# One attention and MLP kernel: the halves of the first MLP tiles placed block by block, and all order tables remade

## The chip, the cores and the metric

The kernel runs on one core of one Trainium2 chip. The metric is the time of one execution on the device, in microseconds. Each core has TensorE (PE, matmuls and transposes; PEld is its weight load), VectorE (DVE), ScalarE (ACT), GpSimd (POOL) and SyncE (SP, which here only issues DMAs). Each engine works through its own instructions strictly in order, and waits for others by semaphores.

## What is computed

```python
# attention: q, k, v (2, 8, 768, 64), centroids (8, 16, 64)
q_assign = argmax(q_n . c_n); k_assign = argmax(k_n . c_n)      # nearest of 16 centroids, by cosine
scores = where(q_assign == k_assign, q . k / 8, -1e9)
x = softmax(scores) @ v                                         # heads side by side: (1536, 512)
# first MLP, weights (512, 2048) and (2048, 512)
h = x @ w_in;  x = (h * cos(h)) @ w_out
# second MLP, weights of the same shapes
h = x @ w_in;  out = where(h > 0, h, exp(min(h, 0)) - 1) @ w_out
```

The MLP weights arrive as 64-bit floats.

## The kernel before, in words

Products of 32-bit precision are made of rounded parts: a value is split into a high half (a copy rounded to the type fp32r that TensorE takes) and a low half (the value less the high half), and a product is the sum of three matmuls, high by high, high by low and low by high.

Attention goes by pairs of heads (8 pairs), each of 12 steps, a step being 128 query rows of one head: 96 steps in all (`NS`). A step n has score matmuls (`qk`, lines 746 and 749, tile s), the row maximum on VectorE (`rowmax`, L754), the exponent on ScalarE (`expo`, L760), six transposes on TensorE (`turn`, L769), the high halves of these on ScalarE (`p_hi`, L783) and the low halves on VectorE (`p_lo`, L789). After three steps twelve value matmuls follow (`av`, L800), which two ScalarE copies (`x_low`, `x_main`, L842 and L853), two GpSimd passes (`x_add`, `x_mul`) and the reciprocal of the row sums (`den_eps`, `recip`, then by way of DRAM `recip_rows` and `recip_out` on SP) turn into x. Beside it the next pair is made ready: transposes of raw q and k (`raw_pe`, L445) and their halves, similarities with the centroids (`sims_pe`, L586, one matmul per 128 rows), sums, a maximum and a first-of-equals (`sims_*`, `best`, `assign` which writes M), and a mask (`mask_pe`, `mask_out`). For the first pair this stands ahead of everything, head by head (`first_*`, L499 to L519; `square` and `sum_sq` for the norms).

An MLP goes by three tiles of 512 tokens (t) and in each by 16 blocks of 128 hidden columns (f). `g1` makes h of a block with 12 matmuls (L203), `act` makes the activation and its halves GH and GL, `g2` adds the block's part to four accumulators with 12 matmuls (L262). In the first tile of each MLP the weights are made too, as `w_part(m, f, i)`: i = 0 a ScalarE pass over the raw words into u (L145), i = 1 a shift and i = 2 a merge on VectorE (L147, L149), i = 4 the high half (`whi`, L82 where ScalarE has it), i = 5 the low half (`wlo`, L157 where GpSimd has it), each of 128x1024. The raw words of a block's weights, 1 MB, come by two DMAs (L130, L132) into the slot that the halves fill later; the first MLP's slots 0 to 4 are loaded in `open_mlp`, 5 to 15 in `close_attention`, which stands behind all of attention in SP's queue. There are two buffers for u, so block f waits for the low half of the block two before it. `act` of the first MLP is: i = 0 h plus a constant on ScalarE (A), i = 2 the remainder on VectorE (R), i = 3 its absolute value on VectorE (`ABS_ON`), i = 4 Sin on ScalarE, i = 5 the product with h on VectorE, i = 6 the high half GH (`GHI_ON`) and i = 7 the low half GL (`GLO_ON`). `finish` takes an accumulator out, and in the second MLP sends it to DRAM.

The order on each engine is that of a list of parts with a time each: the tables `FIRST` (first pair), `PAIR`, `STEP`, `HALF`, `UNIT` (the steady part of attention), `LAST` (the handover from attention to the MLP) and `MLP` give every part a time in steps, the list is sorted by it, and the parts issue their instructions in that order. The times decide nothing but this order. Which engine does a part is read from the tables that end in `_ON`; `OWN` can overrule them for one block:

```python
def place(what, *key):
    return OWN.get((what, *key))
...
copy_on(place("whi", m, f) or WHI_ON[m], slots[m, f][:, 0:WCOLS], f32(w_u[m, f]))
...
if (place("abs", t, f) or ABS_ON[min(t, 1)]) == "act":
    nc.scalar.activation(out=R, in_=R, func=AF.Abs)
```

Before, `OWN` is empty: in the first tile of the first MLP ScalarE makes all weight high halves and GH, GpSimd all weight low halves and GL, VectorE all absolute values; in that of the second MLP GpSimd makes GH as well.

Of the kernel before, what the change touches and what calls it, by code (L numbers as in the profile page):

```python
# [27 lines left out]
UNIT = {'den_eps': 3.395449, 'recip': 4.382076, 'recip_rows': 7.427179, 'recip_out': 8.211055, 'x_add': 9.795484, 'x_mul': 13.848315}  # L30
LAST = {'open_mlp': (-10.431815,), 'x_hi': (-9.514192, -7.034133, -2.555486, -10.023157), 'x_lo': (-8.047097, -4.932345, -0.617305, -2.950232), 'w_part:0': (-9.420448, -8.609347, -8.290691, -5.915885, -5.184987, -2.504884), 'w_part:1': (-8.653788, -6.829189, -4.664081, -3.78072, -2.797147, -1.733981), 'w_part:2': (-2.317206, -1.232418, -0.87148, -0.600955, 0.212419, 3.118759), 'w_part:3': (-0.448697, 0.124409, 0.564191, 2.438164, 2.488768, 4.597908), 'g1': (-0.307886, 1.731051, 4.372541, 5.094428), 'close_attention': (5.33528,), 'act:0': (0.747785, 0.837811, 1.046582, 2.277094, 3.196946, 3.362042, 3.445046, 4.730737), 'act:1': (2.594399, 2.876142, 3.118762, 3.599105, 4.068132, 4.163887, 5.689334, 7.654582), 'act:2': (4.468217, 4.516452, 5.198942, 5.360867, 5.778692, 5.82839, 5.899724, 7.733904), 'act:3': (6.073842, 6.854719, 7.291519, 7.399848, 7.722534, 7.931365, 8.663391, 8.863032), 'g2': (6.668914, 8.520482, 9.303291, 9.815031), 'w_part:4': (2.42712, 2.960527, 3.091453, 3.209423, 3.851579, 6.448056), 'w_part:5': (5.381259, 5.610103, 6.550675, 6.924254, 7.503784, 8.022706), 'w_part:6': (6.555402, 7.031497, 8.030499, 8.308408, 8.684242, 8.926541), 'w_part:7': (9.14231, 9.347017, 9.526266, 9.904052, 10.071843, 10.148753), 'w_part:8': (9.531231, 9.594698, 10.007708, 10.329222, 10.764157, 11.321912), 'w_part:9': (10.67596, 11.080638, 11.588344, 12.058398, 12.098845, 12.307885)}
BASE = 2.147
MLP = ({'w_part:0': -0.40466, 'w_part:1': -0.292589, 'w_part:2': 0.151477, 'w_part:3': 0.670537, 'w_part:4': 0.692693, 'w_part:5': 1.293487, 'g1': 1.795143, 'g2': 5.151129, 'load_w': 11.132613, 'x_hi:0': 1.217665, 'x_lo:0': 1.636338, 'x_hi:1': 0.983316, 'x_lo:1': 1.380274, 'x_hi:2': 0.937158, 'x_lo:2': 1.409528, 'x_hi:3': 0.999253, 'x_lo:3': 1.237302, 'finish:0': 4.421941, 'finish:1': 5.153119, 'finish:2': 4.32082, 'finish:3': 5.26658, 'act:0': 2.239128, 'act:1': 2.366001, 'act:2': 2.377866, 'act:3': 2.492051, 'act:4': 3.000199, 'act:5': 3.084461, 'act:6': 3.139014, 'act:7': 3.424962, 'late_g2:10': 0.47351, 'late_g2:11': 0.529335, 'late_g2:12': 0.229903, 'late_g2:13': -0.690981, 'late_g2:14': -1.391747, 'late_g2:15': -0.882423, 'late_g1:0': 0.043116, 'late_g1:1': -0.794958, 'late_g1:2': -0.713539, 'late_g1:3': 0.294451}, {'w_part:0': -1.966086, 'w_part:1': -1.781932, 'w_part:2': -0.788006, 'w_part:3': -0.687154, 'w_part:4': -0.611143, 'w_part:5': -0.155152, 'g1': 0.285498, 'g2': 4.282268, 'x_hi:0': 1.691513, 'x_lo:0': 1.848892, 'x_hi:1': 0.938852, 'x_lo:1': 1.85853, 'x_hi:2': 1.333847, 'x_lo:2': 2.040859, 'x_hi:3': 0.942491, 'x_lo:3': 1.7925, 'finish:0': 4.212529, 'finish:1': 4.739817, 'finish:2': 5.863002, 'finish:3': 5.213858, 'act:0': 2.365997, 'act:1': 2.670811, 'act:2': 2.797702, 'act:3': 2.855854, 'act:4': 2.922669, 'act:5': 3.098445, 'act:6': 3.341422, 'act:7': 3.474716, 'late_g2:10': -0.3881, 'late_g2:11': -0.322637, 'late_g2:12': 0.583968, 'late_g2:13': -0.381267, 'late_g2:14': -0.649267, 'late_g2:15': -0.687804, 'late_g1:0': 1.985026, 'late_g1:1': 1.123216, 'late_g1:2': 1.16334, 'late_g1:3': 0.760294})
OWN = {}
XLO_ON = {(0, 0): 'pool', (0, 1): 'dve', (0, 2): 'dve', (1, 0): 'dve', (1, 1): 'dve', (1, 2): 'dve'}
GHI_ON = {(0, 0): 'act', (0, 1): 'act', (1, 0): 'pool', (1, 1): 'act'}
GLO_ON = {(0, 0): 'pool', (0, 1): 'pool', (1, 0): 'pool', (1, 1): 'pool'}
RAW_ON = {('k', 0): 'act', ('k', 1): 'dve', ('q', 0): 'act', ('q', 1): 'act'}
HI2_ON = {('k', 0): 'act', ('k', 1): 'act', ('q', 0): 'act', ('q', 1): 'dve'}
ZON = {'z': 'act', 'k': 'act', 'q': 'act'}  # L40
VHI_ON = {0: 'pool', 1: 'pool'}
SS_ON = {'k': 'pool', 'q': 'pool'}
# [13 lines left out]
def kernel(ctx: ExitStack, tc: tile.TileContext, q, k, v, centroids,  # L56
# [229 lines left out]
    with ExitStack() as actx:  # L286
# [724 lines left out]
```

## Time and profile before

| | us |
|---|---|
| median of 3 runs | 809.8 (808.7 to 810.39) |
| the profiled execution | 809.21 |
| its span, first to last instruction | 807.4 |
| busy: PE, PEld | 782.2, 669.3 |
| busy: DVE, ACT, POOL | 465.2, 490.2, 411.3 |

Busy times are of one profiled execution. Matmuls overlap one another and their ends are modelled, so a busy TensorE can still have waited; how much it had to do is seen from the distance of instructions that follow each other without a wait. The stages by time: the first pair's preparation to about 22 us, attention to 277, the first MLP from there (its first matmuls begin at 266.83, between the last steps of attention) and the second to 802.4. The clock of TensorE is given as a share of full speed, 2.4 GHz.

### The profile page before, as it was taken

The page shows a single profiled execution, that of the slowest core. Times are in us where ns is not written, and L with a number is a line of the kernel's source. Part 1 is how long each engine was busy: PE and PEld are TensorE (multiplying, and loading weights), DVE is VectorE, ACT ScalarE, POOL GpSimd, SP SyncE. Part 2 cuts the span into 40 slices and gives each one's busy share as a digit, 9 for nine tenths or more (in the row PEclk, how much of TensorE's full clock was granted, in tenths as well). Part 3 has the DMA queues.
Part 4 walks back from the last instruction along what each step waited for, and adds up shares of the span by engine and source line. Part 5 has one row for each costly group of instructions (what it writes and reads, how often), then busy time and mean ns, then how long its engine had stood idle before and what let it go on. Part 6 is the DMA issues. An engine that isn't in the chain of part 4 may idle for free.

```text
span 807.4 us, 11261 instructions
## 1 busy us (share of the span) xinstructions
PE 782.2 (97%) x4003; PEld 669.3 (83%) x4003; DVE 465.2 (58%) x751; ACT 490.2 (61%) x894; POOL 411.3 (51%) x427
## 2 busy tenths in 40 slices
PE   5999999999998988999999999999999999999997
PEld 4898999999997876888888888888888888888886
DVE  7898899899898767953332443577874111121110
ACT  4798998998999966744433453556563533343332
POOL 3657667667655767942221132379997222123221
PEclk9999999999999998999999999999999999999999
DMA  3645746746736294000000046571000100010001
GB/s 99 148 103 115 182 101 130 176 96 141 173 76 229 64 377 153 1 0 1 1 1 0 1 157 202 178 246 53 1 1 1 52 1 1 0 43 10 0 1 52
DMA packets 62920, 67.99 MB, mean 84 GB/s; under 512 B 30416, under 2 KB 51408, under 8 KB 62864
## 3 DMA queue, kind: packets, MB, share of 16 engines
q1 hardware_dynamic: 62864, 67.28, 29.8%
q8 instruction: 31, 0.51, 0.3%
q14 instruction: 25, 0.20, 0.1%
HBM read 46.17 MB, written 3.19 MB: 61 GB/s over the span
## 4 chain that ended last, share of the span: by engine, by line
PE 81%; DVE 7%; DMA 5%; ACT 3%; POOL 1%; issue 1%; SPq 1%; ACTq 0%; DVEq 0%; POOLq 0%
PE a L262 31%; PE h L203 30%; PE pt L769 6%; PE px L800 5%; PE s L746 3%; PE s L749 3%; DVE m L754 2%; PE pt_sim L586 2%; PE pt_raw L445 1%; DMA raw<-in_moe_w_in_dram 1%; DVE PL L789 1%; DMA R<-row 1%; ACT u L145 1%; POOL slot L157 1%; DMA raw<-in_moe_w_out_dram 1%
## 5 line engine op out<-in xcount | busy, mean ns | idle before, releaser
L245 POOL TENSOR_TENSOR GL<-A,GH 128x512 fp32r<-128x512 f32 x96 | 134.5, 1402 | 271.1 <-ACT GH L82 268.9
L203 PE MATMUL h<-XH,slot 128*128 128x512 f32 x768 | 252.5, 392 | 4.6 <-POOL slot L157 4.4
L203 PEld LDWEIGHTS h<-XH,slot 128*128 128x128 f32 x768 | 145.0, 189 | 36.0 <-POOL slot L157 5.3
L203 PE MATMUL h<-XL,slot 128*128 128x512 f32 x384 | 150.4, 392 | 0.0
L240 DVE SCALAR_TENSOR_TENSOR A<-R,h 128x512 f32<-128x512 f32 x48 | 33.0, 687 | 161.3 <-ACT R L238 151.1
L262 PE MATMUL a<-GH,slot 128*128 128x512 f32 x384 | 125.6, 391 | 0.0
L262 PE MATMUL a<-slot,GH 128*128 128x512 f32 x384 | 118.3, 389 | 0.0
L789 DVE TENSOR_TENSOR PL<-pt,PH 128x384 fp32r<-128x384 f32 x192 | 98.4, 545 | 20.3 <-ACT PH L783 18.7
L82 ACT ACTIVATE GH<-A 128x512 fp32r<-128x512 f32 x80 | 50.5, 631 | 70.4 <-DVE A L234 37.0
L754 DVE TENSOR_REDUCE m<-s 128x1 f32<-128x768 f32 x96 | 91.1, 949 | 3.7 <-PE s L749 2.1
L783 ACT ACTIVATE PH<-pt 128x384 fp32r<-128x384 f32 x192 | 85.8, 494 | 12.1 <-PE pt L769 10.8
L769 PE MATMUL pt<-ident,P 128*128 128x128 f32 x576 | 89.0, 279 | 1.0 <-DVE PL L789 0.7
L760 ACT ACTIVATE P<-s,m 128x768 f32<-128x768 f32 x96 | 87.1, 907 | 3.5 <-DVE m L754 3.1
L157 POOL TENSOR_TENSOR slot<-u,slot 128x1024 fp32r<-128x1024 f32 x32 | 81.0, 2532 | 12.7 <-ACT slot L82 12.5
L262 PEld LDWEIGHTS a<-GH,slot 128*128 128x128 f32 x384 | 72.6, 189 | 15.1
L203 PEld LDWEIGHTS h<-XL,slot 128*128 128x128 f32 x384 | 72.6, 189 | 14.9
L262 PEld LDWEIGHTS a<-slot,GH 128*128 128x128 f32 x384 | 72.1, 188 | 14.9
L769 PEld LDWEIGHTS pt<-ident,P 128*128 128x128 f32 x576 | 66.7, 141 | 11.3 <-DVE PL L789 4.0
L262 PE MATMUL a<-GL,slot 128*128 128x512 f32 x192 | 75.0, 391 | 0.0
L262 PE MATMUL a<-slot,GL 128*128 128x512 f32 x192 | 74.8, 389 | 0.0
L224 DVE SCALAR_TENSOR_TENSOR R<-A,h 128x512 f32<-128x512 f32 x48 | 32.9, 685 | 69.5 <-ACT A L220 69.5
L236 ACT ACTIVATE R<-h 128x512 f32<-128x512 f32 x48 | 28.6, 596 | 66.0 <-PE h L203 65.2
(140 smaller groups left out, 1273.3 us busy)
## 6 DMA issues: line engine op xcount, KB each, us to landing
raw<-in_moe_w_in_dram SPq DMA_DIRECT2D x32, 512.0 KB, 5.8
raw<-in_moe_w_out_dram SPq DMA_DIRECT2D x32, 512.0 KB, 6.6
nat_k<-in_k_dram SPq DMA_DIRECT2D x16, 192.0 KB, 4.2
nat_q<-in_q_dram SPq DMA_DIRECT2D x16, 192.0 KB, 4.2
nat_v<-in_v_dram SPq DMA_DIRECT2D x8, 384.0 KB, 3.6
R<-row SPq DMA_DIRECT2D x32, 96.0 KB, 3.1
out_dram<-o SPq DMA_DIRECT2D x12, 256.0 KB, 2.0
X0k<-hi SPq DMA_DIRECT2D x7, 192.0 KB, 2.6
```

The lines of the kernel that those rows point to most:

```text
L82: nc.scalar.activation(out=out, in_=in_, func=AF.Copy)
L157: eng.tensor_tensor(out=lo, in0=f32(w_u[m, f]), in1=f32(hi), op=ALU.subtract)
L203: nc.tensor.matmul(h, lhsT=a[:, kd, :], rhs=b, start=(kd == 0 and i == 0), stop=(kd == NKD - 1 and i == 2))
L240: nc.vector.scalar_tensor_tensor(out=A, in0=R, scalar=-1.0, in1=h, op0=ALU.add, op1=ALU.max)
L245: eng.tensor_tensor(out=GL, in0=A, in1=f32(GH), op=ALU.subtract)
L262: nc.tensor.matmul(accs[m, t][e], lhsT=a, rhs=b, start=(f == 0 and i == 0), stop=(f == NF - 1 and i == 2))
L754: nc.vector.tensor_reduce(out=m, in_=st[n]["s"][:, :, 0:HW], axis=AX.XY, op=ALU.max, negate=True)
L760: nc.scalar.activation(out=P, in_=st[n]["s"][:, :, 0:HW], func=AF.Exp, bias=st[n]["m"], accum_out=den_all[:, u % NDEN, j, r, 0:1])
L769: nc.tensor.transpose(pt[:, c * 128:(c + 1) * 128], st[n]["P"][:, e, c * 128:(c + 1) * 128], ident)
L783: nc.scalar.activation(out=ph, in_=pt, func=AF.Copy)
L789: nc.vector.tensor_tensor(out=pl, in0=pt, in1=f32(ph), op=ALU.subtract)
L800: nc.tensor.matmul(tx[g][:, 0:HW], lhsT=V2s[pp][:, j, c, :], rhs=halves[g][a][:, c, :], start=(n == 0), stop=(n == 2 * C - 1))
```

## The change

The constants at the head of the file are replaced; no function changes. The same 3196 parts are in the list as before, with other times, so in another order. `OWN` gets 152 entries: for the first tile of each MLP, block by block, the engine of weight halves, of GH and GL and, in the first MLP, of the absolute value and of the halves of x. Counted over the 16 blocks:

| part | before | after |
|---|---|---|
| first MLP, weight high half | 16 ACT | 10 ACT, 4 POOL, 2 DVE |
| first MLP, weight low half | 16 POOL | 5 POOL, 11 DVE |
| first MLP, absolute value | 16 DVE | 10 ACT, 6 DVE |
| first MLP, GH | 16 ACT | 9 ACT, 4 POOL, 3 DVE |
| first MLP, GL | 16 POOL | 5 POOL, 11 DVE |
| first MLP, x high halves (4) | 4 POOL | 3 POOL, 1 DVE |
| second MLP, weight high half | 16 ACT | 8 ACT, 4 POOL, 4 DVE |
| second MLP, weight low half | 16 POOL | 5 POOL, 11 DVE |
| second MLP, GH | 16 POOL | 6 ACT, 5 POOL, 5 DVE |
| second MLP, GL | 16 POOL | 12 POOL, 4 DVE |

Of the diff, whose table lines run to thousands of characters, the entries that matter below, one to a line:

```diff
 FIRST
-'first_pe:k': -58.006119  'first_pe:q': -81.943081      # head 0
+'first_pe:k': -119.9504   'first_pe:q': -100.7692
-'first_low:k': -3.88111   'first_low:q': -1.740567      # head 1
+'first_low:k': -20.6182   'first_low:q': -20.3961
-'assign': -5.883494                                     # head 0
+'assign': -8.8138
...
 PAIR
-'load_nat:v': -1.887999   'values_hi:0': 8.967329   'square:k': 2.145583   'sum_sq:k': 2.805874
+'load_nat:v': 7.4183      'values_hi:0': 7.8125     'square:k': -4.1197    'sum_sq:k': -1.5017
-'raw_out:q:0': 2.506904   'raw_copy:q:0': 2.854778
+'raw_out:q:0': 1.7899     'raw_copy:q:0': 1.6881
...
 UNIT
-'den_eps': 3.395449  'recip': 4.382076  'recip_rows': 7.427179  'recip_out': 8.211055
+'den_eps': 3.1352    'recip': 3.1373    'recip_rows': 6.7511    'recip_out': 8.8623
...
 LAST
-'close_attention': (5.33528,)
+'close_attention': (6.1635,)
...
 MLP, second
-'finish:0': 4.212529, 'finish:1': 4.739817, 'finish:2': 5.863002, 'finish:3': 5.213858
+'finish:0': 4.899, 'finish:1': 5.6062, 'finish:2': 6.0173, 'finish:3': 6.9746
...
-OWN = {}
+OWN = {('xhi', 0, 0, 3): 'pool', ('whi', 0, 0): 'pool', ('wlo', 0, 0): 'pool',
+       ('xhi', 0, 0, 2): 'dve', ('abs', 0, 0): 'act', ('whi', 0, 3): 'dve', ('wlo', 0, 3): 'dve',
+       ('ghi', 0, 0, 0): 'dve', ('glo', 0, 0, 0): 'dve', ('whi', 0, 5): 'act', ('wlo', 0, 5): 'dve',
...
-HI2_ON = {('k', 0): 'act', ('k', 1): 'act', ('q', 0): 'act', ('q', 1): 'dve'}
+HI2_ON = {('k', 0): 'act', ('k', 1): 'act', ('q', 0): 'act', ('q', 1): 'act'}
-SQ0_ON = {('k', 0): 'pool', ('k', 1): 'pool', ('q', 0): 'pool', ('q', 1): 'pool'}
+SQ0_ON = {('k', 0): 'act', ('k', 1): 'act', ('q', 0): 'act', ('q', 1): 'act'}
```

On TensorE the handover is now ordered h1 (among the last transposes), h0, the last twelve value matmuls, h2, h3, a0, h4, a1, h5, a2, h6, h7, a3, a4, h8, a5, h9; before it was h0, h1, the last value matmuls, h2, h3, a0, h4, a1, h5, a2, a3, h6, h7, a4, h8, a5, h9 (h for `g1`, a for `g2` of a block).

## Rows read from the trace of the kernel before

**Rows 1.** Busy us by stretch: span, PE, PEld, DVE, ACT, POOL, clock, DMA share, GB/s.
```profile
237.20:277.00 39.80, 36.70 (x219) 32.44 (x218) 36.29 (x62) 38.73 (x76) 22.13 (x15) 1.00 0.49 149
277.00:315.36 38.36, 33.73 (x133) 26.55 (x133) 25.45 (x32) 25.71 (x35) 28.19 (x16) 0.91 0.86 304
315.36:802.40 487.04, 487.04 (x2149) 403.23 (x2147) 195.35 (x236) 220.96 (x330) 206.39 (x132) 1.00 0.12 40
```

**Rows 2.** Chain that ended last, 195 to 320: start, us, what.
```profile
204.70 0.66 PE pt L769 x6
205.36 1.12 PE px L800 x6
206.48 0.35 PE s L746 x2
...
223.53 1.02 PE pt_sim L586 x10
...
307.39 4.63 PE h L203 x10
312.02 3.50 PE a L262 x12
315.52 2.72 PE h L203 x12
```

**Rows 3.** Timeline, TensorE, the two long waits for a slot.
```profile
293.35 0.73 PE L203 MATMUL h<-XH,slot 128*128 128x512 f32 x2 [2.05 <-POOL slot L157]
...
307.39 1.22 PE L203 MATMUL h<-XH,slot 128*128 128x512 f32 x2 [2.38 <-POOL slot L157]
```

**Rows 4.** Busy us by stretch behind the second wait.
```profile
307.40:312.00 4.60, 4.60 (x11) 3.63 (x12) 3.57 (x4) 3.31 (x4) 4.60 (x3) 0.50 0.81 293
```

**Rows 5.** Timeline, TensorE, the same score matmul of two pairs.
```profile
93.56 0.51 PE L749 MATMUL s<-T0k,T0q 80*128 80x384 f32 x2
...
124.07 0.51 PE L749 MATMUL s<-T0k,T0q 80*128 80x384 f32 x2
```

**Rows 6.** Groups by form, 278 to 318, DVE and POOL: count, busy us, mean ns.
```profile
L149 DVE SCALAR_TENSOR_TENSOR u<-raw,u 128x1024 uint32<-128x1024 uint32 x6 | 8.7, 1455 | 0.0
L229 DVE TENSOR_SCALAR R<-R 128x512 uint32<-128x512 uint32 x7 | 6.1, 872 | 0.1
...
L157 POOL TENSOR_TENSOR slot<-u,slot 128x1024 fp32r<-128x1024 f32 x7 | 19.1, 2726 | 5.8 <-ACT slot L82 5.6
L245 POOL TENSOR_TENSOR GL<-A,GH 128x512 fp32r<-128x512 f32 x7 | 9.6, 1373 | 6.3 <-ACT GH L82 5.6 <-DMA raw<-in_moe_w_out_dram 0.7
```

**Rows 7.** Single lines, whole span: duration ns min/median/max, first and last start.
```profile
L149 DVE SCALAR_TENSOR_TENSOR u<-raw,u x32: 1210/2128/2941, 245.7 to 605.6; 128x1024 uint32<-128x1024 uint32 x32
...
L147 DVE TENSOR_SCALAR u<-u x32: 677/858/1782, 245.0 to 603.0; 128x1024 uint32<-128x1024 uint32 x32
...
L229 DVE TENSOR_SCALAR R<-R x48: 412/428/1859, 273.2 to 532.5; 128x512 uint32<-128x512 uint32 x48
...
L184 DVE TENSOR_TENSOR XL<-X,XH x20: 677/684/2880, 358.7 to 708.7; 128x512 fp32r<-128x512 f32 x20
...
L82 ACT ACTIVATE GH<-A x80: 615/632/634, 279.0 to 794.1; 128x512 fp32r<-128x512 f32 x80
```

**Rows 8.** Single line, the Sin of the first MLP, its table load.
```profile
L232 ACT ACT_TABLE_LOAD  x1: 1283/1283/1283, 276.2 to 276.2; - x1
```

**Rows 9.** Timeline, ScalarE, first pass over slot 5.
```profile
284.10 1.12 ACT L145 ACTIVATE u<-raw 128x1024 f32<-128x1024 f32 x1 [1.36 <-DMA raw<-in_moe_w_out_dram]
```

**Rows 10.** Timeline, the start: M, a low of head 1, scores of n=4.
```profile
17.45 0.36 DVE L652 TENSOR_TENSOR M<-desc,best 128x192 bf16<-128x192 f32 x1
17.84 0.95 DVE L519 SCALAR_TENSOR_TENSOR X1k<-s_raw,T1k 64x768 fp32r<-64x768 f32 x1
...
32.13 0.51 PE L749 MATMUL s<-T0k,T0q 80*128 80x384 f32 x2
```

**Rows 11.** Timeline, ScalarE, the last two finishes.
```profile
802.44 1.08 ACT L279 ACTIVATE o<-a 128x512 f32<-128x512 f32 x2 [0.71 <-PE a L262]
```

More of the change, by code (lines that the diff above doesn't have):

```diff
@@ new lines @@
+STEP = {'qk': -0.9501, 'rowmax': -0.4274, 'expo': 0.9088, 'turn:0': 1.4366, 'p_hi:0': 2.2233, 'p_lo:0': 2.3784, 'turn:1': 1.5744, 'p_hi:1': 2.2522, 'p_lo:1': 2.4943}
+HALF = {'av:0:0': 6.3717, 'av:0:1': 6.6165, 'av:1:0': 4.8239, 'av:1:1': 4.894, 'av:2:0': 5.106, 'av:2:1': 6.5252, 'av:3:0': 6.6157, 'av:3:1': 4.9272, 'av:4:0': 4.8245, 'av:4:1': 4.5762, 'av:5:0': 6.1581, 'av:5:1': 4.9281, 'x_main': 7.7674, 'x_low': 7.2758}
+UNIT = {'den_eps': 3.1352, 'recip': 3.1373, 'recip_rows': 6.7511, 'recip_out': 8.8623, 'x_add': 11.5493, 'x_mul': 19.9117}
@@ new lines @@
+LAST = {'open_mlp': (-11.7232,), 'x_hi': (-6.9932, -9.6535, -10.4, -2.2727), 'x_lo': (-5.2648, -9.0363, -3.2692, -1.1074), 'w_part:0': (-9.3565, -9.0364, -9.03, -5.5193, -5.1072, -3.8309), 'w_part:1': (-7.9318, -7.2433, -5.2706, -4.1975, -2.8769, -1.6649), 'w_part:2': (-4.8385, -4.3951, -1.4472, 0.615, 3.2482, 3.2716), 'w_part:3': (-1.019, 0.5941, 1.6768, 2.5775, 3.777, 4.1252), 'g1': (0.8107, -0.5127, 4.7174, 4.7308), 'close_attention': (6.1635,), 'act:0': (2.0305, 2.3368, 2.3981, 3.3401, 4.2825, 5.0135, 5.7725, 5.7864), 'act:1': (1.4689, 1.51, 1.6084, 2.8969, 2.9091, 4.8262, 7.771, 8.6008), 'act:2': (4.9218, 5.7646, 6.1495, 6.3438, 6.9099, 7.8827, 8.0362, 8.615), 'act:3': (6.6056, 7.0472, 7.9693, 8.6857, 9.0722, 9.1821, 9.8773, 10.6748), 'g2': (6.7732, 8.6124, 9.0089, 10.9244), 'w_part:4': (0.5239, 1.0969, 1.497, 1.6058, 4.7178, 6.0011), 'w_part:5': (6.3413, 6.4575, 7.0319, 7.768, 7.8076, 8.2483), 'w_part:6': (7.325, 7.9776, 8.4162, 9.1286, 9.1532, 9.1532), 'w_part:7': (8.5798, 8.7945, 9.081, 9.1252, 9.1661, 9.7701), 'w_part:8': (10.2246, 10.4313, 10.8014, 11.1405, 11.3903, 11.4335), 'w_part:9': (9.9037, 10.1676, 11.3489, 11.5204, 11.5912, 12.524)}
@@ L32 @@
 BASE = 2.147
-MLP = ({'w_part:0': -0.40466, 'w_part:1': -0.292589, 'w_part:2': 0.151477, 'w_part:3': 0.670537, 'w_part:4': 0.692693, 'w_part:5': 1.293487, 'g1': 1.795143, 'g2': 5.151129, 'load_w': 11.132613, 'x_hi:0': 1.217665, 'x_lo:0': 1.636338, 'x_hi:1': 0.983316, 'x_lo:1': 1.380274, 'x_hi:2': 0.937158, 'x_lo:2': 1.409528, 'x_hi:3': 0.999253, 'x_lo:3': 1.237302, 'finish:0': 4.421941, 'finish:1': 5.153119, 'finish:2': 4.32082, 'finish:3': 5.26658, 'act:0': 2.239128, 'act:1': 2.366001, 'act:2': 2.377866, 'act:3': 2.492051, 'act:4': 3.000199, 'act:5': 3.084461, 'act:6': 3.139014, 'act:7': 3.424962, 'late_g2:10': 0.47351, 'late_g2:11': 0.529335, 'late_g2:12': 0.229903, 'late_g2:13': -0.690981, 'late_g2:14': -1.391747, 'late_g2:15': -0.882423, 'late_g1:0': 0.043116, 'late_g1:1': -0.794958, 'late_g1:2': -0.713539, 'late_g1:3': 0.294451}, {'w_part:0': -1.966086, 'w_part:1': -1.781932, 'w_part:2': -0.788006, 'w_part:3': -0.687154, 'w_part:4': -0.611143, 'w_part:5': -0.155152, 'g1': 0.285498, 'g2': 4.282268, 'x_hi:0': 1.691513, 'x_lo:0': 1.848892, 'x_hi:1': 0.938852, 'x_lo:1': 1.85853, 'x_hi:2': 1.333847, 'x_lo:2': 2.040859, 'x_hi:3': 0.942491, 'x_lo:3': 1.7925, 'finish:0': 4.212529, 'finish:1': 4.739817, 'finish:2': 5.863002, 'finish:3': 5.213858, 'act:0': 2.365997, 'act:1': 2.670811, 'act:2': 2.797702, 'act:3': 2.855854, 'act:4': 2.922669, 'act:5': 3.098445, 'act:6': 3.341422, 'act:7': 3.474716, 'late_g2:10': -0.3881, 'late_g2:11': -0.322637, 'late_g2:12': 0.583968, 'late_g2:13': -0.381267, 'late_g2:14': -0.649267, 'late_g2:15': -0.687804, 'late_g1:0': 1.985026, 'late_g1:1': 1.123216, 'late_g1:2': 1.16334, 'late_g1:3': 0.760294})
@@ L34 @@
-OWN = {}
+MLP = ({'w_part:0': -0.2382, 'w_part:1': -0.0963, 'w_part:2': 0.6148, 'w_part:3': 0.7967, 'w_part:4': 0.948, 'w_part:5': 1.2027, 'g1': 1.7513, 'g2': 5.5344, 'load_w': 8.2327, 'x_hi:0': 0.9527, 'x_lo:0': 1.4768, 'x_hi:1': 1.7284, 'x_lo:1': 1.7874, 'x_hi:2': 1.5925, 'x_lo:2': 1.7606, 'x_hi:3': 1.6825, 'x_lo:3': 2.2845, 'finish:0': 6.1866, 'finish:1': 6.4201, 'finish:2': 6.0872, 'finish:3': 6.3206, 'act:0': 3.5031, 'act:1': 3.5386, 'act:2': 3.6808, 'act:3': 4.0763, 'act:4': 4.2507, 'act:5': 4.6025, 'act:6': 4.6742, 'act:7': 4.7479, 'late_g2:10': -0.2447, 'late_g2:11': 0.4206, 'late_g2:12': -0.0006, 'late_g2:13': 0.0638, 'late_g2:14': 0.0643, 'late_g2:15': 0.2696, 'late_g1:0': 1.2005, 'late_g1:1': 0.6155, 'late_g1:2': -0.3025, 'late_g1:3': 0.2275}, {'w_part:0': -3.59, 'w_part:1': -2.6806, 'w_part:2': -2.3734, 'w_part:3': -2.3145, 'w_part:4': -1.9133, 'w_part:5': -1.8112, 'g1': 1.9042, 'g2': 6.8521, 'x_hi:0': 1.1353, 'x_lo:0': 2.0428, 'x_hi:1': 1.7677, 'x_lo:1': 1.8971, 'x_hi:2': 1.9846, 'x_lo:2': 2.154, 'x_hi:3': 1.2067, 'x_lo:3': 2.1577, 'finish:0': 4.899, 'finish:1': 5.6062, 'finish:2': 6.0173, 'finish:3': 6.9746, 'act:0': 2.7567, 'act:1': 2.9513, 'act:2': 3.2473, 'act:3': 3.4508, 'act:4': 3.5028, 'act:5': 4.2828, 'act:6': 4.3448, 'act:7': 4.4352, 'late_g2:10': -0.4512, 'late_g2:11': -1.0203, 'late_g2:12': -1.6724, 'late_g2:13': -2.2593, 'late_g2:14': -1.3338, 'late_g2:15': -2.0684, 'late_g1:0': 0.6796, 'late_g1:1': 0.5894, 'late_g1:2': 0.2147, 'late_g1:3': 0.132})
```

9 lines of the change are left out of this document (3 added, 6 removed).

## The prediction

> **What bounds the kernel now.** I read the windows by stage first. From 315.36 to 802.4 us TensorE is busy for all of 487.04 us, at clock 1.00, while VectorE, ScalarE and GpSimd are busy 195, 221 and 206 us: nothing that those three do there can shorten the end, only lengthen it [rows 1]. So the change can gain only ahead of 315 us, or after the last matmul. There I compare the time that TensorE took with what its instructions cost back to back, read from the chain: a product block (12 matmuls) 2.72 us, six transposes 0.66, six value matmuls 1.12, two score matmuls 0.35, ten similarity matmuls 1.02 [rows 2].
>
> - Handover, 277.00 to 315.36: 38.36 us [rows 1]. The order there is h2, h3, a0, h4, a1, h5, a2, a3, h6, h7, a4: 11 blocks, 29.9 us. **8.4 us are lost.** Two waits for a weight slot on GpSimd (2.05 and 2.38 us, somewhat more with what the modelled ends hide) are about 5.3 of them [rows 3]. The second is followed by a stretch from 307.4 to 312 at clock 0.50, the lower of the two levels, 1.2 GHz [rows 4]: blocks h7 and a4 took 4.63 + 3.50 us there and not 2.27 + 2.72 (ten and twelve matmuls), 3.1 us [rows 2].
> - End of attention, 237.2 to 277.0: 84 transposes, 66 value, 45 score and 24 h matmuls are 9.2 + 12.3 + 7.9 + 5.4 = 34.9 us of 39.8, so 4.9 lost. ScalarE is busy 38.73 us of it, VectorE 36.29 [rows 1]: ScalarE binds, VectorE stands right behind.
> - One pair of heads: 124.07 - 93.56 = 30.51 us between like score matmuls [rows 5]. Work: 48 score, 72 + 12 transposes, 48 value, 24 similarity and a mask: 8.4 + 9.2 + 9.0 + 2.4 + 0.5 = 29.5. Lost 1.0, seven times over.
>
> **The change, part by part.** No instruction is added or taken away except that Abs is an activation in 10 cases; all else is who does it, and in which order.
>
> *Weight and activation halves in the first MLP tile.* Per block f, GpSimd made a weight low half (2.73 us) and an activation low half (1.37), ScalarE a weight high half [rows 6]. Now VectorE makes 11 of 16 weight low halves. The trace has none there; the nearest row is VectorE's 128x1024 pass with two inputs in SBUF, 1.21 us at its fastest, 2.94 at its slowest [rows 7]; I take 1.21 and keep 2.94 as the far end. On the path of a slot that is 1.5 us less for each. 11 activation low halves go to VectorE at 0.68 (the same operation on x, [rows 7]), against 1.37. Abs on ScalarE is a pass of 128x512, as GH is, 0.63 us [rows 7], against 0.41 to 1.86 on VectorE. It could cost more if it needed a table: the load ahead of the first Sin took 1.28 us, once for 48 Sins with Identity, Copy and Prelu between them [rows 8]. So between 0 and 2 x 1.28 for each Abs; I take 0, since four kinds share that table.
>
> Load per block afterwards, by the fastest rows: VectorE 0.68 + 1.21 (weights) + 2 x 0.68 (products) + 0.41 x 6/16 + 1.21 x 11/16 + 0.68 x 11/16 + 0.15 (few high halves at 0.68) = 4.9 us; GpSimd 1.3 x 4/16 + 2.73 x 5/16 + 0.65 x 4/16 + 1.37 x 5/16 = 1.8 (high halves there not shown; between half of and all of a low half; I take half); ScalarE 3.9. TensorE needs 5.44 for a block of both products. VectorE is thus at 90%, and becomes the second most loaded engine.
>
> Does slot 5 come in time? Its first pass on ScalarE waited for the data until 284.10 [rows 9]. On SP the loads of slots 5 on stand behind the last reciprocal rows, written and read back. In the new order the last reciprocal is taken right after the denominators and not a step later behind a weight pass (1.2), so the loads can leave some 1.2 us sooner, at most a step (2.5) sooner; if not, as now. From 282.5 or 284 on: first pass 1.1, shift 0.7 and merge 1.2 with product work between them, high half about 1.1 as the first pass, low half 1.21: ready at 289.4 to 291. TensorE needs it after h4 and a1, at 290.4, where it was served at 293.3 [rows 3]. Slot 7, served at 307.39, is then due at 298.5 and ready near 296.3; slots 8 and 9 come within a microsecond of their due time by the same count. So the waits go; next late are slots 8 and 9, on VectorE. I let 1.6 of the 8.4 us stay: **-6.8** (bounds -8.4, and -1 if the low halves cost their far end: 1.2 us a block more, 0.65 over 5.44, 11 times). With no wait of over 2 us the clock should hold.
>
> *End of attention.* Four weight high halves (4 x 1.06) leave ScalarE for GpSimd and VectorE: 38.7 falls to 34.4 (1.06 is GH's 0.63 with twice the columns, less a start of 0.2). VectorE gains one x half, one high and one low half (0.4 + 0.7 + 1.2, by its one- and two-input rows [rows 7]): 38.6. So VectorE binds 1.2 us below the 39.8 now: **-1.0** (-3 to 0).
>
> *Order in the pairs.* Core order on each engine (scores n, row max n, exponent n-1, transposes n-2) is as before. The value matmuls go 5, 6, 1 over three steps and not 6, 6, 0, which fills one idle spot (0.2 us). Against that two x copies and two raw copies (each below GH's 0.63; about 0.5 for its 384 columns of 512) now stand together ahead of one exponent, where they stood in two steps: that exponent comes up to 1 us later. The v load is issued on SP behind the reciprocal rows, just ahead of its use: GpSimd's v copies wait for it, behind them stand the next pair's squares, and VectorE's sum of these 2.5 steps (6.4 us) on waits if they are late, with row max and low halves queued behind it. How long the v load takes there no row of before shows; I take it as covered by the 6.4 us and keep a miss in the far end. **0**, with -3.5 (half of what is lost) to +7 (1 us a pair).
>
> *Start.* ScalarE takes four squares from GpSimd, and the second head's lows and similarities move ahead of the first steps. M, at 17.45, comes some 1.9 us later: four lows of 0.95 stand ahead of it on VectorE, not two [rows 10]. But the second head's chain, which stood between the first steps, is then done, and ScalarE's exponents follow each other from there. I put the score matmuls of n=4, at 32.13 [rows 10], 1 us sooner: **-1.0** (-2.5, twice a low and more, to +1.9, if M's delay stays).
>
> *Second MLP's first tile.* Before it TensorE had no gap, and it gets lighter on GpSimd (16 low and 16 GH passes fall to 5 and 5): **0**, hidden by 5.44 us of TensorE per block; without that cover, VectorE's 3.9 us per block would show first.
>
> *End.* The finishes ran 0, 1, 3, 2: the two last, 1.08 us together, both followed the last matmul, after 0.71 us of waiting [rows 11]. Now 2 goes before 3 and fills that wait: **-0.5**.
>
> **Sum.** -6.8 - 1.0 + 0 - 1.0 + 0 - 0.5 = -9.3. The profiled execution took 809.21 us (span 807.4, 1.8 around it); the median is 809.8, inside the same spread. From the median: **800.5**.
>
> **Rivals.**
> A. *VectorE becomes the bound of the first tile, because it and GpSimd lengthen each other.* For: the merge pass takes 1.21 us alone but 1.46 in the mean in the handover and up to 2.94, Abs 0.87 against 0.41 [rows 6, 7]. More of VectorE's work is now of this kind. If all of GpSimd's 1.8 us adds to VectorE's 4.9, a block takes 6.7, 1.3 over TensorE's 5.44; over the 11 blocks from slot 5 on that is 14 us. It decides where VectorE's mean per block passes 5.44 us. Then the handover loses 14 and not 8.4 and the rest gains 2.5: 809.8 + 5.6 - 2.5 = 812.9. Against: GpSimd's load falls from 4.1 to 1.8 per block; the lengthening seen now, 0.25 us on the merge and 0.46 on Abs, scaled by that and doubled for the larger share of such work, gives 0.6, so 5.5: just at the limit. Chance 0.08. A rule of the Trainium skill speaks for this rival (SBUF — State Buffer, section Who interferes with whom): a VectorE pass with two SBUF inputs and a GpSimd pass that reads SBUF exclude each other, the later one blocked until the first ends; by it a block would cost between 4.9 and 6.7 us, by how often they meet. The trace agrees in kind (2.94 against 1.21 for the same pass); how often, it does not tell.
> B. *The pairs get longer*, by the lump ahead of one exponent or by the late v load: 0.5 to 1.0 us, seven times, +3.5 to +7: about 805.5. For: the exponent of that step gates the scores two steps on, through two score tiles. Against: similarities now stand ahead of those scores on TensorE and fill. Chance 0.13.
> C. *Loads set slot 5*, issued as late as now, and each later slot follows at transfer speed: half of the handover's loss stays: 803. Chance 0.11.
> D. *Pairs and end of attention give more* (-3.5 and -3): 795. Chance 0.10.
>
> **How the numbers follow.** The forecast (796.5 to 804) has 0.58. The range leaves out A and the far end of D: 794 to 808. This kernel's measurement tells 0.2%, 1.6 us, from no change. Faster: the forecast, C, D and nearly all of B: 0.88. Same, mostly from B: 0.05. Slower, nearly all A: 0.07.
>
> **What would show it.** In the new profile: no wait of TensorE for a slot over 1 us after 277 and no stretch at clock 0.50 near 307 (handover); the block order reached 315's place 7 us earlier; VectorE above ScalarE in the end of attention; like scores 30.5 us apart (pairs); M near 19.4 and n=4 by 31.5 (start); one finish after the last matmul (end); three table loads in all (Abs). I am wrong if VectorE's low halves take near 2.9 us, if the pairs are over 31.2 us apart, or if TensorE, full from 315 on now, shows gaps in the second MLP.

## The result, and the profile after

The kernel after takes **795.32 us** (median of 4 runs, 795.26 to 795.55), the one before 809.58 beside it (808.7 to 810.39): a ratio of 0.9825, 95% interval 0.9808 to 0.9842, so 14.3 us or 1.75% less. The forecast was 800.5, range 794 to 808: right in sign and inside the range, 5 us short in size. The profiled execution after took 795.37 us, its span 793.6, 13.8 less than before.

Of the page of the kernel after, the busy times and the granted clock: TensorE is busy 98% of the span and its clock stays at the upper level in all 40 slices, as it did not before [rows 4].

```profile
PE 775.6 (98%) x4003; PEld 668.1 (84%) x4003; DVE 501.8 (63%) x792; ACT 481.1 (61%) x894; POOL 325.5 (41%) x386
...
PEclk9999999999999999999999999999999999999999
```

Windows of the kernel after: the end of attention, the handover (from h2 to h8) and the rest to the last matmul, with the columns of [rows 1].

```profile
233.20:272.98 39.78, 36.51 (x221) 32.62 (x220) 37.78 (x62) 35.83 (x73) 21.98 (x17) 1.00 0.52 149
272.98:302.93 29.95, 29.95 (x134) 24.78 (x133) 28.96 (x36) 23.54 (x31) 7.41 (x6) 1.00 1.06 375
302.93:789.50 486.57, 486.57 (x2148) 402.80 (x2147) 225.07 (x274) 213.37 (x332) 144.30 (x104) 1.00 0.12 40
```

h2 to h8 took 38.36 us before (277.00 to 315.36, [rows 1]); now it takes 29.95, which is eleven blocks of 2.72 and nothing else, 8.4 us less. (The 38.52 and 8.6 in an expectation below take one end from the timeline and the other from the chain, which puts the same block 0.16 us later.) In return VectorE is busy 28.96 of those 29.95 us and GpSimd only 7.41. The chain of waits after (start, us, what) shows the same: its last wait for another engine ends at 257.25, where before it ended at 307.39 [rows 2].

```profile
257.25 0.55 PE pt L769 x3
...
272.98 5.46 PE h L203 x24
278.45 2.72 PE a L262 x12
...
297.49 5.44 PE a L262 x24
302.93 2.72 PE h L203 x12
```

The weight low halves after, both MLPs (ns min/median/max, first and last start): 1.22 us in the median on VectorE, 2.41 on GpSimd.

```profile
L157 DVE TENSOR_TENSOR slot<-u,slot x22: 1209/1217/2045, 274.1 to 576.9; 128x1024 fp32r<-128x1024 f32 x22
L157 POOL TENSOR_TENSOR slot<-u,slot x10: 2387/2410/2897, 244.2 to 582.3; 128x1024 fp32r<-128x1024 f32 x10
```

Timeline after, ScalarE's first pass over slot 5, which answers to [rows 9]: no wait for the data, and 5.5 us sooner, 4.2 of them by attention's lead.

```profile
278.56 1.15 ACT L145 ACTIVATE u<-raw 128x1024 f32<-128x1024 f32 x1
```

Timeline after, TensorE: the scores of n=4 and like scores of two pairs. Beside [rows 5, 10] n=4 comes 1.44 us sooner, and the period is 30.26 us, not 30.51.

```profile
30.69 0.52 PE L749 MATMUL s<-T0k,T0q 80*128 80x384 f32 x2
...
91.57 0.52 PE L749 MATMUL s<-T0k,T0q 80*128 80x384 f32 x2
...
121.83 0.52 PE L749 MATMUL s<-T0k,T0q 80*128 80x384 f32 x2
```

Timeline after, ScalarE, the last two finishes: the first of the two fills what was a wait in [rows 11], and only the last stands behind the last matmul, which starts at 789.42.

```profile
789.16 1.28 ACT L279 ACTIVATE o<-a 128x512 f32<-128x512 f32 x2
```

Where the 13.8 us went, by the starts of like instructions in the two timelines (before and after: n=76 215.78 and 212.78, h2 277.01 and 272.82, h8 315.36 and 302.76, the last matmul 802.02 and 789.42):

| stretch | forecast | measured |
|---|---|---|
| start to the scores of n=4 | -1.0 | -1.4 |
| pairs, n=4 to n=76 | 0 | -1.6 |
| end of attention, n=76 to h2 | -1.0 | -1.2 |
| handover, h2 to h8 | -6.8 | -8.4 |
| h8 to the last matmul | 0 | 0.0 |
| end | -0.5 | -1.2 |
| sum | -9.3 | -13.8 |

### The profile page after: what moved, and what is told of

The parts are those of the page before. It is cut to its first block, busy times and chain, and to the rows that moved or that the text cites. A ratio compares the mean times of both kernels' runs of the same rounds, so it can differ in the third digit from the quotient of the medians.

```text
span 793.6 us, 11239 instructions
## 1 busy us (share of the span) xinstructions
PE 775.6 (98%) x4003; PEld 668.1 (84%) x4003; DVE 501.8 (63%) x792; ACT 481.1 (61%) x894; POOL 325.5 (41%) x386
## 4 chain that ended last, share of the span: by engine, by line
PE 88%; DVE 7%; ACT 3%; issue 1%; POOL 1%; DMA 0%; ACTq 0%
PE h L203 33%; PE a L262 33%; PE px L800 7%; PE pt L769 6%; PE s L746 3%; PE s L749 3%; DVE PL L789 2%; DVE m L754 2%; PE pt_sim L586 2%; PE pt_raw L445 1%; ACT Z L681 1%; ACT PH L783 1%; ACT P L760 0%; PE pt_mask L660 0%; PE s_raw L499 0%
## 5 line engine op out<-in xcount | busy, mean ns | idle before, releaser
L203 PE MATMUL h<-XH,slot 128*128 128x512 f32 x768 | 249.6, 389 | 0.0
L245 POOL TENSOR_TENSOR GL<-A,GH 128x512 fp32r<-128x512 f32 x81 | 112.2, 1386 | 316.5 <-ACT GH L82 271.9
L232 ACT ACTIVATE R<-R,cbias 128x512 f32<-128x512 f32 x48 | 34.7, 724 | 47.3 <-DVE R L229 47.1
L800 PE MATMUL px<-PL,V 128*128 128x384 f32 x192 | 59.8, 365 | 1.7 <-DVE ss L558 0.3
```

Source lines behind the costliest of these rows:

```text
L203: nc.tensor.matmul(h, lhsT=a[:, kd, :], rhs=b, start=(kd == 0 and i == 0), stop=(kd == NKD - 1 and i == 2))
L232: nc.scalar.activation(out=R, in_=R, func=AF.Sin, scale=-2.0 * PI, bias=cbias[:, 1:2])
L245: eng.tensor_tensor(out=GL, in0=A, in1=f32(GH), op=ALU.subtract)
L800: nc.tensor.matmul(tx[g][:, 0:HW], lhsT=V2s[pp][:, j, c, :], rhs=halves[g][a][:, c, :], start=(n == 0), stop=(n == 2 * C - 1))
```

## The experiments

All hybrids are made by exchanging tables or single entries between the two kernels. Times are medians; each ratio is to the kernel before, run beside it on the same chip (808.2 to 809.2 there).

### Parts of the change alone, in the kernel before

**e1_handover**

```diff
-LAST, MLP, OWN of the kernel before
+LAST, MLP, OWN of the kernel after
```

> The kernel before with three tables of the one after: LAST, MLP and OWN (handover, both MLPs and the placement); all of attention, its reciprocals and the start as before. My theory: the handover's gain (38.52 us from h2 to h8 before, 29.95 after: 8.6) comes from these tables alone, and the end's 1.2 with it: 809.6 - 8.6 - 1.2 = 799.8, no wait for a slot over 1 us and clock 1.00 throughout. Rival (loads set slot 5): the first load of slot 5 left 7.7 us sooner in the kernel after, 4.0 of it by attention's lead and 3.7 because the reciprocals are earlier in its UNIT table; without that table slot 5 comes up to 3.7 us late: one wait for a slot of 1 to 3.7 us, 801 to 803.5.

811.41 us, ratio 1.0028 (1.0013 to 1.0043): slower, and both theories fell. The handover itself came near what it is in the kernel after (h2 to h8 in 31.3 us, 287.36 to 318.62), but h2 started 10.4 us later than before. What holds it is a chain over four engines. GpSimd's timeline in e1_handover: an x_mul (L867) waits 3.02 us for its reciprocal rows, with a weight low half queued behind it.

```profile
255.36 1.11 POOL L867 TENSOR_TENSOR X<-X,R 128x384 f32<-128x384 f32 x1 [3.02 <-DMA R<-row]
256.43 2.35 POOL L157 TENSOR_TENSOR slot<-u,slot 128x1024 fp32r<-128x1024 f32 x1
```

ScalarE's timeline: the next weight pass waits for that low half, and attention's copies stand behind it.

```profile
258.82 1.12 ACT L145 ACTIVATE u<-raw 128x1024 f32<-128x1024 f32 x1 [4.17 <-POOL slot L157]
```

TensorE's timeline: two waits for low halves of attention, 7.84 us together.

```profile
262.09 0.90 PE L769 MATMUL pt<-ident,P 128*128 128x128 f32 x3 [4.78 <-DVE PL L789]
...
283.38 0.66 PE L800 MATMUL px<-PL,V 128*128 128x384 f32 x1 [3.06 <-DVE PL L789]
```

Behind each wait TensorE's clock was at the lower level, 1.2 GHz: 0.52 from 262.0 to 265.4 us and 0.51 from 283.3 to 289.5. The second wait is of the same kind as the first: the low half stands in VectorE's list behind a pass of the activation (L224, 280.95), which had waited 1.48 us for ScalarE.

**e5_handover_xmul**

```diff
 # e1_handover, and
-UNIT: 'x_add': 9.795484, 'x_mul': 13.848315
+UNIT: 'x_add': 11.5493,  'x_mul': 19.9117
```

> The kernel before with LAST, MLP and OWN of the one after (as in e1_handover) and, of UNIT, the times of x_add and x_mul alone. In e1_handover the two x_mul passes on GpSimd stood ahead of a weight low half: the first waited 3.02 us for its reciprocal rows, the low half ended at 258.8, ScalarE's next weight pass had waited 4.17 us for it, and TensorE lost 4.78 us at 262. My theory: with x_mul behind the low halves that wait goes and 4 to 5 us with it, from 809.6 to 805 (span); the 3.06 us wait for the last low half of attention at 283 stays, it has another cause. Rival: something else on ScalarE or VectorE holds the same pass: within 1 us of e1_handover.

810.95 us, 1.0032 (1.0018 to 1.0046). TensorE's timeline in e5_handover_xmul: the 4.78 us wait fell to 2.47, the other stayed as expected.

```profile
262.99 0.55 PE L769 MATMUL pt<-ident,P 128*128 128x128 f32 x3 [2.47 <-DVE PL L789]
...
282.70 0.66 PE L800 MATMUL px<-PL,V 128*128 128x384 f32 x1 [3.05 <-DVE PL L789]
```

The place of x_mul and x_add was thus about half of that wait. But the steady pairs paid: the row maximum of n=76 came 1.3 us later than before, with 6.1 us of waiting of TensorE for M in place of 2.9. The span fell by 1.2 us against e1_handover and not by 4.6. `UNIT` holds for every pair, so a pass put behind the low halves at the end of attention moves in all of them.

**e2_start** and **e3_pairs**

```diff
 # e2_start
-FIRST, SQ0_ON, HI2_ON of the kernel before
+FIRST, SQ0_ON, HI2_ON of the kernel after
 # e3_pairs
-PAIR, STEP, HALF, UNIT of the kernel before
+PAIR, STEP, HALF, UNIT of the kernel after
```

> The kernel before with FIRST, SQ0_ON and HI2_ON of the one after (the first pair alone). If the start's lead (score matmuls of n=4 at 30.7 and not 32.1) is carried to the end: 809.6 - 1.4 = 808.2. Rival: the steady pairs swallow it (in the kernel after the lead was 0.8 at n=16): 808.8 to 809.6.

> The kernel before with PAIR, STEP, HALF and UNIT of the one after (steady attention alone). If these tables alone shorten the pairs: like scores 30.25 and not 30.51 us apart, lead of 1.6 at n=76 and 3.0 at n=88, less the 0.4 that the last steps gave back, and slots loaded sooner: 806 to 807. By the prediction's step (pairs 0): 809.6. Rival: the gain needs the new start or the new handover tables as well: 808.5 to 809.6.

e2_start took 811.66 us, 1.0038 (1.0020 to 1.0057); e3_pairs 820.98, 1.0144 (1.0121 to 1.0166). No theory had either slower. The row maximum of n=8, at 44.02 before, came at 47.08 and 50.86: each set of tables alone makes the first steps late. But TensorE's timeline in e3_pairs shows like scores 30.19 us apart, twice:

```profile
100.09 0.51 PE L749 MATMUL s<-T0k,T0q 80*128 80x384 f32 x2
...
130.28 0.51 PE L749 MATMUL s<-T0k,T0q 80*128 80x384 f32 x2
...
160.47 0.52 PE L749 MATMUL s<-T0k,T0q 80*128 80x384 f32 x2
```

So the steady tables alone do shorten a pair, by 0.3 us; e6_attention gives them the start that belongs to them. The start is not all: at the row maximum of n=95 e3_pairs was 4.9 us late, at h2 9.7 (286.67 against 277.01), so half was lost where these pairs meet the handover of before.

**e6_attention**

```diff
-FIRST, PAIR, STEP, HALF, UNIT, SQ0_ON, HI2_ON of the kernel before
+FIRST, PAIR, STEP, HALF, UNIT, SQ0_ON, HI2_ON of the kernel after
```

> The kernel before with all of attention's tables of the one after (FIRST, PAIR, STEP, HALF, UNIT, SQ0_ON, HI2_ON), handover and MLPs as before, OWN empty. Each half alone was slower (start +0.4%, pairs +1.4%). My theory: the two belong together, since the first steps of the pairs stand between the parts of the second head: together the row maximum of n=76 comes some 4.5 us sooner, as in the kernel after. If the handover takes that lead on: 808.8 - 4 = 804.8. Rival: the handover's parts of before stand in the wrong places between these attention parts, as the other way round in e1_handover, and 2 to 10 us go there: 806.5 to 815.

810.93 us, 1.0032 (1.0020 to 1.0044). Start and pairs do belong together: the row maximum of n=76 came 4.2 us sooner (4.7 in the kernel after). Then the rival held: at n=95 1.8 us of it were left. TensorE's timeline in e6_attention has a new wait at the last value matmuls, and the handover's two old ones, as in [rows 3].

```profile
275.06 0.41 PE L800 MATMUL px<-PL,V 128*128 128x384 f32 x1 [1.96 <-DVE PL L789]
...
296.59 0.73 PE L203 MATMUL h<-XH,slot 128*128 128x512 f32 x2 [1.70 <-POOL slot L157]
...
310.62 0.73 PE L203 MATMUL h<-XH,slot 128*128 128x512 f32 x2 [2.38 <-POOL slot L157]
```

**e4_finish**

```diff
-'finish:2': 5.863002, 'finish:3': 5.213858
+'finish:2': 5.213858, 'finish:3': 5.863002
```

> The kernel before with the second MLP's finishes in the order 0, 1, 2, 3 and not 0, 1, 3, 2; nothing else. By the prediction's step one finish stands behind the last matmul and not two: -0.5, 809.1. Rival, from the trace after (span 3.8 us past the last matmul and not 5.0): the last two output transfers no longer leave together, which is worth 0.7 more: -1.2, 808.4.

809.44 us, 1.0006 (0.9992 to 1.0019): too small for the measurement. The profiles tell more. From the start of the last matmul to the end of the span, the six profiles with the finishes 0, 1, 3, 2 have 5.38 (before), 5.05 and four of 4.76 to 4.79; the eight with 0, 1, 2, 3 have 5.12 (this one), 4.56 and six of 4.13 to 4.19. By the medians the order is worth 0.6 us, near the 0.5 forecast; the other 0.6 of the 1.2 is a slow transfer in that one profile of before (2.8 us to land, 2.1 in the median of its last four). That two transfers leaving together cost 0.7 is not shown.

### Placement and order against each other

**e7_placement** and **e12_low_before**

```diff
 # e7_placement: the kernel before, with
-OWN = {}
+OWN of the kernel after
 # e12_low_before: the kernel before, with
-OWN = {}
+OWN = {('wlo', 0, f): 'dve' for f in (3, 4, 5, 6, 7, 8, 10, 11, 12, 14, 15)}
```

> The kernel before, order as before, with the table OWN of the one after. By the prediction's step, in which the engine of the halves is what ends the slot waits: they go, 5 to 8 us: 801 to 804. Rival: in the old order the passes that now stand in VectorE's queue hold back what was listed for it there (row maxima, low halves of attention, remainders), and the gain is used up by that: 806 or more, with new waits for VectorE.

> The kernel before, order as before, with one edit: the eleven weight low halves that OWN gives to VectorE are there, all else on its old engine. By the prediction's step (each slot 1.5 us sooner, VectorE busy 25.5 of 38.4 us in the handover): the two waits of 2 us go, and the low clock behind them: 800 to 803. Rival, after e7_placement (14.5 us slower, 11 us of waits for low halves on VectorE): in the old order the low half stands behind the remainder and the product of other blocks, is later than on GpSimd, and holds those back in turn: 809 to 815.

822.75 us, 1.0181 (1.0161 to 1.0202), and 815.49, 1.0074 (1.0050 to 1.0098). In both the rival held (e12_low_before came out 0.5 us above its range). TensorE's waits in e7_placement (us in total, times, longest):

```profile
PE h L203 <- DVE slot L157: 11.0, 8, 2.5
```

In e12_low_before, one edit, the first of these waits can be followed. ScalarE's timeline: the high half of block 3 was done at 275.94.

```profile
274.88 1.06 ACT L82 ACTIVATE slot<-u 128x1024 fp32r<-128x1024 f32 x1
```

VectorE's timeline: its low half takes only 1.22 us, but stands in the list behind the product of block 1 (L234), which waited for ScalarE's Sin until 281.68.

```profile
281.68 0.69 DVE L234 TENSOR_TENSOR A<-h,R 128x512 f32<-128x512 f32 x1 [1.93 <-ACT R L232]
282.29 1.22 DVE L157 TENSOR_TENSOR slot<-u,slot 128x1024 fp32r<-128x1024 f32 x1
```

TensorE's timeline: h3 waits.

```profile
283.56 0.73 PE L203 MATMUL h<-XH,slot 128*128 128x512 f32 x2 [2.72 <-DVE slot L157]
```

Behind this wait the clock stayed at 1.00 (283.5 to 287.0), so a wait of over 2 us need not lower it. In the kernel before GpSimd made this half from 275.54 to 278.75. It took 3.2 us, but in a queue where nothing of the activation stood ahead of it. The kernel after lists block 3's low half (time 100.13 in the tables) ahead of block 1's product (100.83); before it was the other way round (100.60 and 100.16). The loss is not in the handover alone: from h2 to h8 e12_low_before even took 37.2 us (277.48 to 314.65), 1.2 less than the kernel before, and then 7.5 more from h8 to the last matmul, with five waits for low halves there (5.6 us).

**e8_order**, **e9_low_back**, **e10_glo_back** and **e11_abs_back**

```diff
 # the kernel after, first MLP's first tile, with
 # e9_low_back
-('wlo', 0, f): 'dve'      # f = 3, 4, 6, 7, 8, 10, 11, 12, 14, 15
+('wlo', 0, f): 'pool'
 # e10_glo_back
-('glo', 0, 0, f): 'dve'   # eleven blocks
+('glo', 0, 0, f): 'pool'
 # e11_abs_back
-('abs', 0, f): 'act'      # ten blocks
+('abs', 0, f): 'dve'
 # e8_order: all three
```

> The kernel after, order as after, with the engines of before for ten of the eleven weight low halves, all activation low halves and all absolute values of the first MLP's first tile (GpSimd, GpSimd, VectorE); high halves, the low half of block 5 and the second MLP's placement stay as after. If placement carries the handover: waits for slots on GpSimd of 2 us and more come back and the clock falls behind them: 795.3 + 5 to 9 = 800 to 804. Rival (order and the earlier loads carry it): within 1.5 us of 795.3.

> The kernel after with ten of its eleven VectorE weight low halves of the first MLP back on GpSimd (block 5 stays); nothing else. In the kernel after a slot is done only 0.4 to 2.6 us ahead of its first matmul in the handover, and a low half takes 1.21 us on VectorE and 2.4 to 2.85 on GpSimd. My theory (the engine of the low half is the step that paid): waits for slots on GpSimd of 1 to 2 us come back, 3 to 8 us: 798.5 to 803.5. Rival (what failed in e8_order were the activation low halves, or the three kinds only together): under 1.5 us from 795.3.

> The kernel after with all activation low halves (GL) of the first MLP's first tile on GpSimd; nothing else. VectorE, busy 28.96 of 29.95 us in the handover, gets 0.68 lighter for each of eleven, GpSimd, busy 7.41, 1.4 heavier. If VectorE's load is what is scarce and GpSimd has room: within 1 us of 795.3. Rival (a pass in GpSimd's order is late for its product block, as the 5.5 us of waiting for GL in e8_order): 3 to 8 us more, 798.5 to 803.5.

> The kernel after with all absolute values on VectorE as before; nothing else. That adds 0.42 us (up to 0.87) for each of ten to VectorE, six of them in the handover, where it has 1.0 us idle: if VectorE binds there (rival A of the prediction stood at this edge): 1.5 to 4 us, 797 to 799.5. If the slots' lead of 0.4 to 2.6 us takes it: 795.3.

| | us | ratio to before | over the kernel after | of it in the profile: h2 to h8, behind h8 |
|---|---|---|---|---|
| e9_low_back | 807.38 | 0.9973 (0.9957 to 0.9989) | +12.1 | 4.0, 6.6 |
| e10_glo_back | 798.27 | 0.9865 (0.9842 to 0.9887) | +3.0 | 1.2, 1.6 |
| e11_abs_back | 798.42 | 0.9864 (0.9841 to 0.9886) | +3.1 | 1.2, 1.9 |
| e8_order | 814.03 | 1.0070 (1.0053 to 1.0088) | +18.7 | 7.3, 10.4 |

The three add up: 12.1 + 3.0 + 3.1 = 18.2 against 18.7 for all. The kernel after did not run beside them; by the ratios to before the four are 12.0, 3.2, 3.2 and 19.8, each good to about 2 us, so the sum holds within that. In the new order each kind of move pays; with the old engines for these three kinds that order is slower than the kernel before. More than half of each loss stands behind h8 (the kernel after takes 486.66 us from there to the last matmul), all of it in the first MLP's first tile: behind 380 us none of the four waits for a slot or a half. For e9 and e8 the theory had the sign and too small a size. Why a low half that takes 1.2 us more costs so much, GpSimd's timeline in e9_low_back shows: a second low half now stands ahead of block 1's GH (281.28, against 276.01 in the kernel after), and with it and an x_add ahead its GL is late too.

```profile
278.46 2.86 POOL L157 TENSOR_TENSOR slot<-u,slot 128x1024 fp32r<-128x1024 f32 x1
281.28 1.07 POOL L86 TENSOR_SCALAR GH<-A 128x512 fp32r<-128x512 f32 x1
282.31 1.98 POOL L861 TENSOR_TENSOR X<-X,xt 128x384 f32<-128x384 f32 x1
284.25 1.27 POOL L245 TENSOR_TENSOR GL<-A,GH 128x512 fp32r<-128x512 f32 x1
```

ScalarE's timeline: its next activation waits for that GL, and the weight passes of the next slots stand behind it.

```profile
285.56 0.69 ACT L220 ACTIVATE A<-h,cbias 128x512 f32<-128x512 f32 x1 [4.17 <-POOL GL L245]
```

In the kernel after this GL ends at 280.99. For e11 the theory that VectorE binds held (1.5 to 4 us forecast, 3.1 measured). Its window of the handover: VectorE busy for all but 0.41 of 30 us, and TensorE no longer full.

```profile
273.00:303.00 30.00, 29.59 (x128) 23.61 (x128) 29.59 (x39) 20.68 (x26) 6.46 (x5) 1.00 1.05 375
```

For e10 neither theory held cleanly. From 273 to 333 us seven GL passes left VectorE, which had taken 5.5 us of it in the kernel after, but its busy time fell by 2.99 us only. The window of the kernel after, and below it of e10_glo_back:

```profile
273.00:333.00 60.00, 60.00 (x266) 49.65 (x266) 58.28 (x70) 45.91 (x60) 21.18 (x12) 1.00 0.54 191
```

```profile
273.00:333.00 60.00, 59.20 (x261) 48.53 (x260) 55.29 (x60) 44.39 (x58) 30.12 (x19) 1.00 0.54 191
```

Ten passes fewer are in the window, three of them because the kernel ran later; several kinds of those that stayed got longer. By form, 273 to 333 us, the merge and the absolute value in the kernel after and then in e10_glo_back (count, busy us, mean ns):

```profile
L149 DVE SCALAR_TENSOR_TENSOR u<-raw,u 128x1024 uint32<-128x1024 uint32 x11 | 15.7, 1426 | 0.1
...
L229 DVE TENSOR_SCALAR R<-R 128x512 uint32<-128x512 uint32 x4 | 1.7, 415 | 0.0
```

```profile
L149 DVE SCALAR_TENSOR_TENSOR u<-raw,u 128x1024 uint32<-128x1024 uint32 x10 | 16.1, 1609 | 0.1
...
L229 DVE TENSOR_SCALAR R<-R 128x512 uint32<-128x512 uint32 x4 | 3.7, 918 | 0.0
```

## Why the prediction was right, and where it was not

- **What bounds the kernel: right.** From h8 to the last matmul nothing changed (486.66 us in both), the second MLP's first tile included, and nearly all of the gain came from ahead of it. That the other engines can only lengthen this stretch held too: e9_low_back took 493.3 us for it.
- **Handover, -6.8: too small by 1.6, and right in mechanism for the new order only.** The price of the low half on VectorE, 1.21 us from the merge pass, was met (1.22), the data of slot 5 came in time, and no wait for a slot and no low clock are left. The term that was mis-sized is "I let 1.6 of the 8.4 us stay": all 8.4 went. But "on the path of a slot that is 1.5 us less for each" takes the engine alone; in the old order the same move cost 6.3 us (e12_low_before), because the pass then waits in VectorE's list.
- **Loads of slot 5: too late in the forecast, and rival C fell.** They left at 270.44 and not 278.10; of the 7.7 us, 4.2 are attention's lead and 3.5 the order, where the forecast had 1.2, at most 2.5. Early loads alone do not end the waits: in e6_attention they left at 270.48, 9.5 us ahead of h2, and both slot waits stayed. Whether the handover needs the 3.5 us was not tried.
- **VectorE's load: too low.** The prediction has 4.9 us per block. From 273 to 333 us VectorE was busy 58.28 of 60, which is 5.28 for each 5.44: passes lengthened (merges took 1.43 us in the mean, not 1.21). That lies between the 4.9 and the 5.5 of rival A: the kernel came within 0.16 us per block of the point from which that rival decides. An absolute value on VectorE, 0.42 us more in a block, is over it by that count (5.70), and e11_abs_back, with ten of them, was 3.1 us slower.
- **Abs "I take 0": right as a price, wrong as a worth.** Abs took 0.63 us on ScalarE and there are still three table loads. But what it takes off VectorE is worth 3.1 us (e11_abs_back).
- **Pairs, 0: wrong, -1.6.** A pair takes 30.26 us, so rival B, longer pairs, fell; the steady tables alone give 30.19 (e3_pairs). Which of their moves does it was not tried.
- **End of attention, -1.0: right (-1.2).** VectorE is the busier of the two there now (37.78 us of 39.78, ScalarE 35.83), though the forecast had 38.6 and 34.4.
- **Start, -1.0:** -1.4. M came 1.0 us later than before, at 18.42, and not near 19.4.
- **End, -0.5:** right by like with like (0.6); the 1.2 between the two profiles holds a slow transfer of the one before.
- **Rival D** named the time, 795, but not the way: it had pairs at -3.5 and the end of attention at -3, and they gave -1.6 and -1.2.

What the prediction did not see is that its steps are no separate terms. It priced each as if the others stood still. On the chip the handover's tables alone, the start's, the pairs', all of attention's, the placement's and the low halves' alone made the kernel 0.3 to 1.8% slower. In e1_handover and e12_low_before the traces show why: a part held up on one engine holds all that is listed behind it there; for the others this is the likely cause and was not followed from pass to pass. The sum came out because the tables fit one another when all are taken together; that was not argued in the prediction, only assumed. How the 8.4 us of the handover divide between order and placement has no answer in these runs: with either alone the time is above that of before.

## What to carry to other kernels

A pass moved to a faster engine comes sooner only if nothing late stands ahead of it in that engine's list: read what is queued there before counting its duration, and move it in the order too. Where order and placement are made together, forecast them together, from the time that the bounding engine loses in a stage, and don't judge one by trying it without the other. Count the busy time per block of the engine that takes the work: at 5.28 us of 5.44, ten passes of 0.42 us more were worth 3 us.

## What the runs showed of the hardware

VectorE and GpSimd can make one another wait for a whole pass. VectorE's and GpSimd's timelines in the kernel after, at the place where it shows best:

```profile
277.80 2.04 DVE L157 TENSOR_TENSOR slot<-u,slot 128x1024 fp32r<-128x1024 f32 x1
```

```profile
277.52 1.24 POOL L861 TENSOR_TENSOR X<-X,xt 128x384 f32<-128x384 f32 x1 [0.89 <-ACT X L853]
278.71 2.28 POOL L245 TENSOR_TENSOR GL<-A,GH 128x512 fp32r<-128x512 f32 x1
```

VectorE's pass starts under GpSimd's first and ends 1.08 us after it (at 279.84), near its 1.21 alone; GpSimd's second starts under VectorE's and ends 1.15 us after that (at 280.99), near its 1.28 alone. So each seems to have waited for the other's pass to end. The absolute value, with its one input in SBUF, lengthens too: 0.41 to 1.86 us [rows 7]. Not all passes do this. Those that read h from PSUM and one tile from SBUF keep their time even where GpSimd is busy most, as e8_order shows (GpSimd busy 43 of 60 us from 273 to 333):

```profile
L234 DVE TENSOR_TENSOR A<-h,R x48: 677/691/693, 274.4 to 545.4; 128x512 f32<-128x512 f32 x48
```

The Trainium skill (SBUF — State Buffer, section Who interferes with whom) says this of VectorE passes with two SBUF inputs against GpSimd passes that read SBUF, and says that a VectorE pass with at most one SBUF input, outside the modes that use both ports, is free of it. The trace agrees in both, with 2.04 against 1.21 us for the one kind and 0.69 throughout for the other.

The scatter of the times was not expected either. The kernel after, e10_glo_back and e11_abs_back, in which TensorE hardly waits behind 257 us, stay within 0.3, 1.0 and 0.6 us over 4 to 6 runs; all other hybrids spread over more, from 1.9 us in 6 runs (e8_order) to 5.4 us in 12 (e1_handover). No run here shows the reason.
